# Low parts of w1 and w2 as identity products on TensorE, first score masks on VectorE

## The chip, the cores and the metric

One core of one Trainium2 chip. The metric is the device time of one execution in microseconds (us). Engines are called PE (TensorE), DVE (VectorE), ACT (ScalarE), POOL (GpSimd) and SP (SyncE, which issues loads here). Each engine works through its own queue in order.

## The reference

The input passes three stages: a gated linear attention with the delta rule, a gated product of matrices, and a soft mixture of eight experts. Cut to what is computed:

```python
k_n = k / (np.linalg.norm(k, axis=-1, keepdims=True) + 1e-06)
for t in range(S):                       # S = 768, batch 4, 8 heads, head size 48
    y[:, :, t] = einsum('bhd,bhde->bhe', q[:, :, t], state)
    v_old = einsum('bhde,bhd->bhe', state, k_n[:, :, t])
    state = state + beta[:, :, t] * einsum('bhd,bhe->bhde', k_n[:, :, t], v[:, :, t] - v_old)
x = y.transpose(0, 2, 1, 3).reshape(3072, 384)
x = ((x @ w1) * (x @ w2)) @ w3 @ w_out   # w1, w2: 384 x 1024; w3: 1024 x 1024; w_out: 1024 x 384
logits = x @ phi                         # 32 slots
slots = softmax(logits, 0).T @ x         # 4 slots for each of 8 experts
out = softmax(logits, 1) @ experts(slots)   # relu(s @ w1[e]) @ w2[e]
```

The weights w1, w2, w3 and w_out are float64.

## The kernel before, in words

**Attention.** The sequence is cut into 24 pieces of 32 positions (n), two to a pair (p), four to a solve (s). For a solve, PE makes the Gram products of the keys (`g_step`, L428), DVE masks them into `dg` (L373), transposes them (L454), takes the norms by Newton steps (L461 to L480) and inverts the 32x32 triangles by columns (L520 and L523 for the solves 0 and 1, which invert two halves of 16 and join them with PE, `join2`). `ends[s]` is the last transpose into W (L533). The score products of queries with keys go to PSUM too; `g_evac` masks them into the tile `kl`. For n below PP = 16, ACT copies the part that is masked to SBUF (`praw`, L384), POOL multiplies by the mask (L393, L400), and ACT copies four strips directly (L408). For later n, DVE masks straight from PSUM in the same lines. `chain_steps` is then the recurrence of piece n: v times norms on POOL (`pre`, L585), `ks` (L599), `vv` (L610), `yy` (L620), the state products (L630), and `xt`, which turns the result into `xT`, a high and a low part in fp32r (L645, L646).

**Weights.** The float64 values are loaded as pairs of integers (L279). `to_f32` rebuilds float32: DVE takes the exponent (L290), ACT scales it (L291), DVE puts in the sign (L292), makes the mantissa (L294, L296), and POOL multiplies the two (L299). For w1 and w2 (w12, eight blocks of 128x768, `w12_steps`) ACT casts the high part (L306) and POOL (blocks 0, 3, 6) or DVE (the others) subtracts it from the whole (L307) to give the low part. Four blocks can lie raw in SBUF, in two slots of the tile `gx` and two of `raw`; the whole has two slots (NT12). w_out and w3 go the same way in pieces of 384 or 256 columns, through the tile `hold`, with transposes on PE.

**Main.** `prod` (L695) multiplies xT by w1 and w2 in blocks f of 128 columns, 18 products of 128x256 each, `ab`; ACT copies one half (L699), DVE multiplies (L704). Logits, softmax and the sums over slots follow for each pair of pieces, then the experts.

**Order.** Steps are put down with a time (`when`, `spread`, with shifts by label in SHIFT); they are traced in order of these times, and a scheduler that simulates the engines then fixes the order of each queue. `tc.issue_after(x)` queues what is traced in its block behind x on x's own engine; it adds no wait, and does nothing to other engines' queues. An engine that waits at one instruction holds up all behind it. The PSUM banks for scores of solve 1 and for the products `ab` are the same two.

Of the kernel before, what the change touches and what calls it, by code (L numbers as in the profile page):

```python
# [42 lines left out]
DR = 0.3  # L43
NU = 2
NUG = 10
TW0 = 0.05
TW1 = 0.8
CL = 1.0
NW = 3
# [3 lines left out]
J1 = (0.8, 1.2, 1.8, 2.0)  # L53
NT12 = 2
# [7 lines left out]
LT = 1.799  # L62
LTS = 0.311
JAT = (1, 2, 3)
PP = 16
LAST = 1
EA = 11.73
JO = (-0.7, 0.1, 0.2)
G1 = -0.341
# [16 lines left out]
GA = (0.2, -0.09)  # L86
# [34 lines left out]
def kern(ctx, tc, kq, vt, kt, bl, w12, w3, wo, phi, w1e, w2e, consts, out):  # L121
# [44 lines left out]
    spr = pc.tile([128, 2, 2, 2, 32], F32R, name="spr")  # L166
    row = pc.tile([1, 32], F32, name="row")
# [74 lines left out]
    def load(p, which="kq"):  # L242
# [6 lines left out]
        SP.dma_start(out=t[64:112, 4 - i:7:2, :], in_=kq[p][64:112, 1 - i::2])  # L249
        SP.dma_start(out=t[0:64, i:4:2, :], in_=kq[p][0:64, i::2])  # L250
# [15 lines left out]
    turn, last_v = [0], []  # L266
# [15 lines left out]
    def to_f32(r, n, name):  # L282
# [79 lines left out]
    Dg = {}  # L362
# [47 lines left out]
    def g_step(n, hs, which="gp"):  # L410
# [12 lines left out]
        for h in hs:  # L423
            for b in range(4):
# [3 lines left out]
                T.matmul(gp[trow(n, b), h - hs[0]], lhsT=t[r, k[j], kc], rhs=t[r, slots, kc], start=True, stop=True)  # L428
# [6 lines left out]
        g_evac(n, hs, gp, blocks, n < PP)  # L435
# [838 lines left out]
```

## Time and profile before

| | |
|---|---|
| three runs | 642.67, 645.42, 648.51 us; median 645.42 |
| profiled execution | span 640.7 us from first to last instruction (its own time is not given beside it) |
| busy | PE 548.9 us (86%), DVE 400.3 (62%), ACT 278.6 (43%), POOL 161.8 (25%) |
| products `ab` (L695) | 1728 instructions, 247.1 us busy |
| chain of waits that ended last | PE 55%, DVE 26%, issue 6%, DMA 5%, POOL 4%, ACT 3% of the span |

The busy times are means over the whole span. The chain of waits is followed back from the last instruction: what ended each wait, or what stood ahead on the same engine. The rows below are read by stage. A time in a timeline row is the start from the first instruction, then the length of what is merged in the row; the last number is how many instructions are merged.

### The profile page before, as it was taken

Reading aid. Unit: us, or ns where it says so; the run is one execution under the profiler, and the core shown is the slowest. Engines: PE = TensorE matmul, PEld = TensorE weight load, DVE = VectorE, ACT = ScalarE, POOL = GpSimd, SP = SyncE. Lnnn points to the kernel's source line nnn. Section 1 sums busy time; section 2 is a strip of 40 time slices with the busy share of each in tenths; the row PEclk is TensorE's granted clock in tenths of the full one; section 3 lists DMA queues with packets and bytes.
Section 4 is the critical chain, followed back from the end, with each engine's and each line's share of the span. In section 5 each row is a group of like instructions: output and inputs, shape, how many; then the busy total and the mean of one; then the engine's idle time right before and its main releaser. Section 6 shows DMA issues by size and latency. Waiting matters only on the chain.

```text
span 640.7 us, 25996 instructions
## 1 busy us (share of the span) xinstructions
PE 548.9 (86%) x11417; PEld 458.8 (72%) x11417; DVE 400.3 (62%) x1257; ACT 278.6 (43%) x704; POOL 161.8 (25%) x215
## 2 busy tenths in 40 slices
PE   5324546888899799899999999897999999999996
PEld 4323435887777688679888888786989899886464
DVE  3996899998667115994379826997982313134124
ACT  1515644245574436454444455343444454333023
POOL 0726858334254016232030113004010000000100
PEclk9999666598999989999999999999999999999997
DMA  9904234446843720310404030122344130788848
GB/s 205 332 4 146 81 83 144 130 130 204 254 151 129 164 70 17 87 45 18 105 7 96 9 90 30 38 61 63 106 145 155 63 108 2 268 274 318 344 160 265
DMA packets 36945, 81.72 MB, mean 128 GB/s; under 512 B 4352, under 2 KB 17792, under 8 KB 35584
## 3 DMA queue, kind: packets, MB, share of 16 engines
q1 hardware_dynamic: 36832, 80.07, 40.9%
q8 instruction: 89, 1.46, 1.0%
q14 instruction: 24, 0.20, 0.1%
HBM read 69.57 MB, written 10.49 MB: 125 GB/s over the span
## 4 chain that ended last, share of the span: by engine, by line
PE 55%; DVE 26%; issue 6%; DMA 5%; POOL 4%; ACT 3%; SPq 0%; DVEq 0%; POOLq 0%; ACTq 0%
PE ab L695 24%; DMA kl<-kq 4%; PE gp L712 3%; PE yp L620 3%; DVE xl L512 2%; PE vp L610 2%; DVE tmp L509 2%; PE sacc L630 2%; PE gp L428 2%; PE ks L599 2%; PE sacc L1119 2%; PE hp L1098 2%; DVE gl L454 2%; DVE xl L487 1%; PE lp L719 1%
## 5 line engine op out<-in xcount | busy, mean ns | idle before, releaser
L695 PE MATMUL ab<-xT,wsl 128*128 128x256 f32 x1728 | 247.1, 296 | 3.6 <-DVE gT L704 2.2
L695 PEld LDWEIGHTS ab<-xT,wsl 128*128 128x128 f32 x1728 | 221.8, 196 | 15.6 <-issue 6.3
L704 DVE TENSOR_TENSOR gT<-ab,bs 128x256 f32<-128x256 f32 x84 | 35.2, 422 | 87.3 <-ACT bs L699 79.0
L699 ACT COPY bs<-ab 128x256 f32<-128x256 f32 x96 | 35.7, 371 | 68.0 <-PE ab L695 66.3
L585 POOL TENSOR_TENSOR v<-v,nnT 128x384 f32<-128x384 f32 x24 | 21.4, 894 | 139.2 <-DMA v<-vt 57.0
L575 ACT COPY sv<-vp 32x384 f32<-32x384 f32 x96 | 45.1, 470 | 16.2 <-PE vp L610 14.5
L512 DVE TENSOR_TENSOR xl<-xl,tmp 128x84 f32<-128x84 f32 (+35 forms) x220 | 51.5, 266 | 0.7
L509 DVE TENSOR_TENSOR tmp<-xl 128x84 f32<-128x84 f32 (+35 forms) x220 | 49.6, 259 | 0.4
L428 PE MATMUL gp<-kl 48*32 48x64 f32 (+1 forms) x1024 | 35.7, 275 | 11.7 <-ACT kl L408 8.6
L299 POOL TENSOR_TENSOR hold<-hold 128x384 f32<-128x384 f32 (+1 forms) x32 | 32.7, 1025 | 47.9 <-DVE hold L296 23.0
L428 PEld LDWEIGHTS gp<-kl 48*32 48x32 f32 x1024 | 26.1, 121 | 17.8 <-ACT kl L408 8.9
L713 ACT COPY gtok<-gp 128x512 f32<-128x512 f32 x48 | 28.2, 588 | 17.2 <-PE gp L712 15.0
L393 POOL TENSOR_TENSOR kl<-praw,cs 64x256 f32<-64x256 f32 x28 | 25.3, 903 | 33.5 <-ACT praw L384 32.3
L620 PE MATMUL yp<-sv,kl 112*32 112x48 f32 (+2 forms) x1280 | 26.3, 215 | 7.6 <-ACT sv L575 7.6
L291 ACT ACTIVATE hold<-hold,cs 128x384 int32<-128x384 int32 (+1 forms) x32 | 18.7, 589 | 27.7 <-DVE hold L290 27.3
L408 ACT COPY kl<-gp 32x256 f32<-32x256 f32 x64 | 23.2, 363 | 15.0 <-DVE kl L393 11.8
L620 PEld LDWEIGHTS yp<-sv,kl 112*32 112x32 f32 (+2 forms) x1280 | 20.4, 115 | 12.2 <-issue 8.4
L610 PE MATMUL vp<-v,w 32*32 32x48 f32 x1536 | 25.3, 207 | 3.1 <-DVE mst L738 0.9
L646 DVE TENSOR_TENSOR xT<-xp,xT 128x384 fp32r<-128x384 f32 x24 | 13.3, 553 | 22.8 <-ACT xT L645 22.6
L610 PEld LDWEIGHTS vp<-v,w 32*32 32x32 f32 x1536 | 20.1, 107 | 10.2 <-issue 6.0
L712 PE MATMUL gp<-cs,gT 128*128 128x128 f32 x168 | 26.9, 279 | 0.0
L400 POOL TENSOR_TENSOR kl<-praw,cs 32x256 f32<-32x256 f32 x28 | 23.2, 828 | 7.7 <-ACT praw L384 4.8
(248 smaller groups left out, 980.6 us busy)
## 6 DMA issues: line engine op xcount, KB each, us to landing
hold<-w SPq DMA_DIRECT2D x16, 384.0 KB, 3.3
v<-vt SPq DMA_DIRECT2D x24, 192.0 KB, 2.7
kk<-kt SPq DMA_DIRECT2D x12, 384.0 KB, 6.7
unitg<-w1e SPq DMA_DIRECT2D x6, 768.0 KB, 5.7
kl<-kq SPq DMA_DIRECT2D x8, 512.0 KB, 6.8
kl<-kq SPq DMA_DIRECT2D x8, 384.0 KB, 4.6
gx<-w SPq DMA_DIRECT2D x4, 768.0 KB, 8.2
raw_w<-w SPq DMA_DIRECT2D x4, 768.0 KB, 8.8
```

Source lines behind the costliest of these rows:

```text
L299: G.tensor_tensor(out=w, in0=m, in1=w, op=ALU.mult)
L428: T.matmul(gp[trow(n, b), h - hs[0]], lhsT=t[r, k[j], kc], rhs=t[r, slots, kc], start=True, stop=True)
L509: V.tensor_tensor(out=tmp[:, 0:n, lo:hi], in0=x[:, j + 1:32, j:j + 1].to_broadcast([128, n, hi - lo]), in1=x[:, j:j + 1, lo:hi].to_broadca ...
L512: V.tensor_tensor(out=x[:, j + 1:32, lo:hi], in0=x[:, j + 1:32, lo:hi], in1=tmp[:, 0:n, lo:hi], op=ALU.add)
L575: A.copy(o, i)
L610: T.matmul(p[o, h * D:(h + 1) * D], lhsT=w[o, 8 * n4 + h, :], rhs=r[o, h, :], start=True, stop=True, tile_position=(o.start, o.start))
L620: T.matmul(p[qrow(b), h * D:(h + 1) * D], lhsT=kl[r, (6, 0)[b // 2] if t2 else (4, 2)[b // 2], kcol(h, b)], rhs=sv[r, b, h * D:(h + 1) * D ...
L695: T.matmul(o, lhsT=w[:, m, k], rhs=x[:, k], start=(n == 0), stop=(n == 8))
L699: A.copy(bs, p[:, 256:512])
L704: V.tensor_tensor(out=gt, in0=p[:, 0:256], in1=bs, op=ALU.mult)
L712: T.transpose(p[:, t * 256 + i * 128:t * 256 + (i + 1) * 128], gt[:, t * 128:(t + 1) * 128], ident)
L713: A.copy(gk, p)
```

## The change

- `w12_steps`: the low part is no longer a subtraction. PE multiplies the whole by an identity and the high part by a negative identity (`nid`) into one PSUM bank, half a block at a time, and ACT copies the bank to the low part as fp32r.
- `to_f32`: for w12, the multiplication of blocks 0, 1, 2, 4 and 5 is done by DVE, that of 3, 6, 7 by POOL (`WG`); three blocks instead of two start together behind the first inverse (`AHEAD`), and the whole has four slots (NT12).
- Scores of the pieces 0 to 3 (`PV`) are masked by DVE from PSUM, without the copy by ACT; their steps get own times (`P0`), those after the inverse behind `solved`, the last scaling of the inverse.
- The keys of pairs 0 and 1 are loaded first, pair 1 by ACT's queue; constants and beta follow. Queries, v and the first `kk` are put down inside a block `issue_after` the last Gram product; `pre` inside one behind `solved[0]`.
- Scratch for dynamic DMA is set to 1024, and numbers that set the order are changed.

```diff
-DR = 0.3
+DR = 0.223
...
-TW0 = 0.05
+TW0 = 0.41
...
-J1 = (0.8, 1.2, 1.8, 2.0)
-NT12 = 2
+J1 = (0.8, 0.924, 1.8, 2.0)
+NT12 = 4
+AHEAD = 3
+W0 = -1.0
+W1 = -0.8
+WG = (3, 6, 7)
+PV = (0, 1, 2, 3)
+P0 = (-8.466, -0.99, -0.8, -0.6)
...
-    def to_f32(r, n, name):
+    def to_f32(r, n, name, E=G):
...
-        G.tensor_tensor(out=w, in0=m, in1=w, op=ALU.mult)
+        last_m.append(E.tensor_tensor(out=w, in0=m, in1=w, op=ALU.mult))
...
-            w = to_f32(raw_load(w12[f], 768, f"w{f}"), 768, f"w{f}")
+            w = to_f32(raw_load(w12[f], 768, f"w{f}"), 768, f"w{f}", G if f in WG else V)
             hi, lo = (wsl[f][:, i].rearrange("p m k c -> p (m k c)") for i in range(2))
             A.copy(hi, w)
-            (G if f % NW == 0 else V).tensor_tensor(out=lo, in0=w, in1=hi.bitcast(F32), op=ALU.subtract)
+            for i in range(2):
+                c = slice(384 * i, 384 * i + 384)
+                p = tr(f"lo{f}{i}")[:, 0:384]
+                T.matmul(p, lhsT=ident, rhs=w[:, c], start=True, stop=False)
+                T.matmul(p, lhsT=nid, rhs=hi[:, c], start=False, stop=True)
+                A.copy(lo[:, c], p)
...
-        g_evac(n, hs, gp, blocks, n < PP)
+        g_evac(n, hs, gp, blocks, n < PP and n not in PV)
...
+            with tc.issue_after(solved[0].ins):
+                G.tensor_tensor(out=v, in0=v, in1=nnT[s][:, 8 * n4:8 * n4 + 8].unsqueeze(2).to_broadcast([128, H, D]),
+                                op=ALU.mult)
...
-    when(-9.0, lambda: SP.dma_start(out=cs, in_=consts), *[lambda p=p: load(p, "k") for p in range(2)], lambda: load_b(0),
-         lambda: load(0, "q"), lambda: load_v(0), lambda: load_v(1), lambda: load(1, "q"), lambda: load_kk(0))
+    when(-9.0, lambda: load(0, "k"), lambda: load(1, "k", A), lambda: SP.dma_start(out=cs, in_=consts), lambda: load_b(0))
+    when(-8.89, behind_g0(lambda: load(0, "q"), lambda: load_v(0), lambda: load_v(1), lambda: load(1, "q"), lambda: load_kk(0)))
...
-    spread(-1.0, -0.8, [behind_w12(f, i - 2) for i, f in enumerate(w12s)], "w12")
+    spread(W0, W1, [behind_w12(f, i - AHEAD) for i, f in enumerate(w12s)], "w12")
...
-    nc = bacc.Bacc("TRN2", target_bir_lowering=False, num_devices=1)
+    nc = bacc.Bacc("TRN2", target_bir_lowering=False, num_devices=1, dynamic_dma_scratch_size=1024)
```

How instructions move on three queues. First SP, from its first load on, before; in brackets the semaphores that an instruction waits for (a DMAHW one is the landing of an earlier load):

```order
L862 DMA cs<-consts 128x419
L249 DMA kl_111<-kq 48x2x512
L250 DMA kl_111<-kq 64x2x512
L249 DMA kl_112<-kq 48x2x512
L250 DMA kl_112<-kq 64x2x512
L262 DMA beta_120<-bl 128x32
L249 DMA kl_111<-kq 48x2x512
L250 DMA kl_111<-kq 64x2x512
L254 DMA v_124<-vt 128x384 [waits DMAHW0_49]
```

SP with the change (`kl_112` is the tile of pair 0, `kl_113` of pair 1; line 256 and 257 are `load`):

```order
L256 DMA kl_112<-kq 48x2x512
L257 DMA kl_112<-kq 64x2x512
L891 DMA cs<-consts 128x419
L269 DMA beta_121<-bl 128x32
L256 DMA kl_112<-kq 48x2x512
L257 DMA kl_112<-kq 64x2x512
L261 DMA v_277<-vt 128x384 [waits DMAHW0_49]
L261 DMA v_279<-vt 128x384 [waits DMAHW1_49]
```

The keys of pair 1 have left the queue, the constants stand behind the keys of pair 0; the queries (the second pair of rows on `kl_112`) carry no wait, and v waits for the first landing as before.

DVE at the end of the first inverse, before:

```order
L529 TENSOR_TENSOR xf_493<-xl_489,sm_469 128x16x16 x2
L531 STREAM_TRANSPOSE sums<-xf_493 128x16x32
L533 STREAM_TRANSPOSE w_555<-xf_493 128x32x32
L290 TENSOR_SCALAR t_w_632<-gx 128x768
L290 TENSOR_SCALAR t_w_643<-raw_w_641 128x768
L292 SCALAR_TENSOR_TENSOR t_w_632<-gx,t_w_632 128x768
L292 SCALAR_TENSOR_TENSOR t_w_643<-raw_w_641,t_w_643 128x768
L294 TENSOR_SCALAR gx<-gx 128x768
L294 TENSOR_SCALAR raw_w_641<-raw_w_641 128x768
L296 SCALAR_TENSOR_TENSOR gx<-gx 128x768
```

DVE there with the change (L542 is L529 of before, L405 is L393, L297 to L303 are L290 to L296):

```order
L542 TENSOR_TENSOR xf_311<-xl_307,sm_287 128x16x16 x2
L405 TENSOR_TENSOR kl_112<-p_0_444,cs 64x256
L405 TENSOR_TENSOR kl_112<-p_4_467,cs 64x256
L544 STREAM_TRANSPOSE sums<-xf_311 128x16x32
L546 STREAM_TRANSPOSE w_373<-xf_311 128x32x32
L297 TENSOR_SCALAR t_w_533<-gx 128x768
L297 TENSOR_SCALAR t_w_551<-raw_w_549 128x768
L297 TENSOR_SCALAR t_w_570<-raw_w_568 128x768
L405 TENSOR_TENSOR kl_112<-p_0_444,cs 64x256
L405 TENSOR_TENSOR kl_112<-p_4_467,cs 64x256
L299 SCALAR_TENSOR_TENSOR t_w_533<-gx,t_w_533 128x768
L299 SCALAR_TENSOR_TENSOR t_w_551<-raw_w_549,t_w_551 128x768
```

Two masks stand ahead of the inverse's last transposes and two behind the first exponents, and three blocks are opened where two were.

ACT from the cast of block 6 on, before (L575 copies the state, L408 strips of scores, L699 the first half of `ab`):

```order
L306 CAST wsl_106<-t_w_697 128x768
L575 COPY sv<-sacc_110 48x384
L645 CAST xT_0_861<-xp_1186 128x3x128
L291 ACTIVATE hold<-hold,cs 128x384 x4
L306 CAST wsl_107<-t_w_744 128x768
L384 COPY praw_0_1250<-gp_0_1232 64x128 x2
L408 COPY kl_111<-gp_0_1232 32x2x4x32 x4
L384 COPY praw_4_1277<-gp_4_1259 64x128 x2
L408 COPY kl_111<-gp_4_1259 32x2x4x32 x4
L384 COPY praw_0_1324<-gp_0_1290 64x256 x2
L546 COPY t_2_1571<-j_2_1537 128x128
L324 COPY woT_1122<-wot_1118 128x384
```

ACT with the change (L313 is the cast, L319 the copy of a low part, L588 is L575, L396 and L420 are L384 and L408):

```order
L313 CAST wsl_107<-t_w_686 128x768
L298 ACTIVATE hold<-hold,cs 128x384 x2
L313 CAST wsl_108<-t_w_740 128x768
L319 CAST wsl_107<-lo_694 128x384
L319 CAST wsl_107<-lo_698 128x384
L588 COPY sv<-vp_936 32x384 x4
L659 CAST xT_0_973<-xp_975 128x3x128
L319 CAST wsl_108<-lo_748 128x384
L319 CAST wsl_108<-lo_752 128x384
L637 COPY ys_1014<-yp_981 128x384
L396 COPY praw_0_1037<-gp_0_1019 64x128 x2
L420 COPY kl_114<-gp_0_1019 32x2x4x32 x4
```

Between the cast of block 6 and the scores of piece 4 stand the state copies of piece 1 and the result copies now, which stood ahead of the cast before; the scores of pieces 4 and 5, which stood ahead of that cast too, come behind them.

## Rows read from the trace of the kernel before

**Rows 1.** Busy time by stage: stretch, length, then each engine's busy us and instructions.

```profile
41.10:61.80 20.70, 10.42 (x448) 8.92 (x448) 13.92 (x21) 7.87 (x13) 9.59 (x6) 1.00 0.26 88
61.80:102.50 40.70, 19.00 (x521) 15.75 (x522) 36.08 (x42) 24.17 (x52) 29.89 (x20) 0.64 0.28 78
102.50:140.30 37.80, 32.30 (x537) 29.11 (x536) 37.45 (x127) 13.24 (x29) 17.39 (x18) 0.71 0.53 164
140.30:233.00 92.70, 83.58 (x1837) 69.32 (x1837) 55.79 (x139) 46.33 (x113) 30.04 (x32) 0.94 0.56 159
233.00:585.00 352.00, 339.37 (x7027) 294.74 (x7030) 208.89 (x783) 163.46 (x424) 56.33 (x112) 1.00 0.31 92
```

**Rows 2.** Timeline of the first inverse: start, length, engine, line, operation, tiles.

```profile
14.79 1.97 DVE L454 STREAM_TRANSPOSE gl<-dg 128x1024 f32<-128x1024 f32 x1
...
27.03 0.88 DVE L523 TENSOR_TENSOR xl<-xl,sm 128x44 f32<-128x44 f32 x2
...
28.61 3.10 POOL L393 TENSOR_TENSOR kl<-praw,cs 64x256 f32<-64x256 f32 x4
...
34.99 0.33 DVE L523 TENSOR_TENSOR xl<-xl,sm 128x54 f32<-128x54 f32 x2
...
39.22 1.87 DVE L533 STREAM_TRANSPOSE w<-xf 128x1024 f32<-128x1024 f32 x1
```

**Rows 3.** Timeline, first loads on SP and PE's Gram products.

```profile
0.74 0.39 SPq L862 DMA_DIRECT2D cs<-consts  x1
...
13.53 0.70 PE L428 MATMUL g<-kl 48*32 48x32 f32 x35 [3.80 <-issue]
```

**Rows 4.** Timeline of DVE and POOL, conversion of w12.

```profile
40.93 0.54 DVE L290 TENSOR_SCALAR t_w<-gx 128x768 int32<-128x768 int32 x1
...
42.48 0.96 DVE L292 SCALAR_TENSOR_TENSOR t_w<-gx,t_w 128x768 int32<-128x768 int32 x1 [0.55 <-ACT t_w L291]
43.35 0.95 DVE L292 SCALAR_TENSOR_TENSOR t_w<-raw_w,t_w 128x768 int32<-128x768 int32 x1
...
79.03 1.85 POOL L299 TENSOR_TENSOR t_w<-raw_w,t_w 128x768 f32<-128x768 f32 x1
...
79.42 2.27 DVE L292 SCALAR_TENSOR_TENSOR t_w<-raw_w,t_w 128x768 int32<-128x768 int32 x1 [1.06 <-ACT t_w L291]
...
89.43 2.44 DVE L296 SCALAR_TENSOR_TENSOR gx<-gx 128x768 f32<-128x768 uint32 x1
...
97.86 0.95 DVE L307 TENSOR_TENSOR wsl<-t_w,wsl 128x768 fp32r<-128x768 f32 x1
```

**Rows 5.** DVE instructions grouped by shape: busy us, mean ns.

```profile
L393 DVE TENSOR_TENSOR kl<-gp,cs 64x256 f32<-64x256 f32 x12 | 5.0, 416 | 0.2
```

**Rows 6.** Timeline of PE; in brackets the idle time before and its end.

```profile
1.31 2.93 PE L816 MATMUL sacc<-sv 128*128 128x384 f32 x4 [1.31 <-DVE sv L811]
...
47.39 1.51 PE L610 MATMUL vp<-v,w 32*32 32x48 f32 x64 [0.86 <-DVE w L552]
...
98.45 1.93 PE L428 MATMUL gp<-kl 48*32 48x64 f32 x64 [7.87 <-ACT kl L408]
...
102.56 5.04 PE L695 MATMUL ab<-xT,wsl 128*128 128x256 f32 x22
...
302.17 0.88 PE L610 MATMUL vp<-v,w 32*32 32x48 f32 x64
```

**Rows 7.** Timeline of ACT: state copies, a cast of a block, strips of scores.

```profile
75.04 1.95 ACT L575 COPY sv<-vp 32x384 f32<-32x384 f32 x4
...
88.33 0.83 ACT L306 CAST wsl<-t_w 128x768 fp32r<-128x768 f32 x1
...
96.91 1.49 ACT L408 COPY kl<-gp 32x256 f32<-32x256 f32 x4
```

**Rows 8.** Timeline of DVE, first and last instruction of the second inverse.

```profile
103.74 2.04 DVE L454 STREAM_TRANSPOSE gl<-dg 128x1024 f32<-128x1024 f32 x1
...
138.06 1.92 DVE L533 STREAM_TRANSPOSE w<-xf 128x1024 f32<-128x1024 f32 x1
```

More of the change, by code (lines that the diff above doesn't have):

```diff
@@ L61 @@
 GX = 3.912
-LT = 1.799
+LT = 1.693
 LTS = 0.311
@@ L66 @@
 LAST = 1
-EA = 11.73
-JO = (-0.7, 0.1, 0.2)
-G1 = -0.341
+EA = 11.832
+JO = (-0.7, 0.007, 0.216)
+G1 = -0.437
 S1 = -0.015
@@ L85 @@
 L3 = -0.04
-GA = (0.2, -0.09)
+GA = (0.2, -0.052)
 GB = 0.203
@@ L240, in kern, with load @@
     KV, KK, bt = {}, {}, {}
-    def load(p, which="kq"):
+    def load(p, which="kq", E=SP):
         t = kl_of(p)
@@ L248, in load @@
         i = "qk".index(which)
-        SP.dma_start(out=t[64:112, 4 - i:7:2, :], in_=kq[p][64:112, 1 - i::2])
-        SP.dma_start(out=t[0:64, i:4:2, :], in_=kq[p][0:64, i::2])
+        E.dma_start(out=t[64:112, 4 - i:7:2, :], in_=kq[p][64:112, 1 - i::2])
+        E.dma_start(out=t[0:64, i:4:2, :], in_=kq[p][0:64, i::2])
     def load_v(n):
@@ L427, in g_step @@
                 slots = slice(lo, hi) if j == 0 else slice(hi - 1, lo - 1 if lo else None, -1)
-                T.matmul(gp[trow(n, b), h - hs[0]], lhsT=t[r, k[j], kc], rhs=t[r, slots, kc], start=True, stop=True)
+                m = T.matmul(gp[trow(n, b), h - hs[0]], lhsT=t[r, k[j], kc], rhs=t[r, slots, kc], start=True, stop=True)
+        last_g[:] = [m]
         blocks = {}
@@ L440, in g_parts @@
         return [lambda: g_step(2 * p, range(h)), lambda: g_step(2 * p, range(h, H)), lambda: g_step(2 * p + 1, range(H))]
-    W, nnT, ends = {}, {}, {}
+    W, nnT, ends, solved = {}, {}, {}, {}
     joined = {i: {0} for i in HALVES}
@@ L823, in behind0, with behind_x, g @@
         return g
+    def behind_x(f):
+        def g():
+            with tc.issue_after(solved[0].ins):
+                f()
+        return g
     def behind_w12(f, k):
@@ L861, in kern, with behind_g0, g @@
     w12s = w12_steps()
-    when(-9.0, lambda: SP.dma_start(out=cs, in_=consts), *[lambda p=p: load(p, "k") for p in range(2)], lambda: load_b(0),
-         lambda: load(0, "q"), lambda: load_v(0), lambda: load_v(1), lambda: load(1, "q"), lambda: load_kk(0))
+    def behind_g0(*fs):
+        def g():
+            with tc.issue_after(last_g[0].ins):
+                for f in fs:
+                    f()
+        return g
+    when(-9.0, lambda: load(0, "k"), lambda: load(1, "k", A), lambda: SP.dma_start(out=cs, in_=consts), lambda: load_b(0))
+    when(-8.89, behind_g0(lambda: load(0, "q"), lambda: load_v(0), lambda: load_v(1), lambda: load(1, "q"), lambda: load_kk(0)))
     when(-8.95, first)
+    when(-8.95, lambda: A.activation(out=nid, in_=ident, func=AF.Copy, scale=-1.0))
     for i in range(4):
@@ L867, in kern @@
                                              in_=ident4.unsqueeze(1).to_broadcast([128, 2, 32])))
-    spread(-8.9, -8.8, [lambda n=n: g_step(n, range(H), "g") for n in range(4)], "G0")
+    spread(-8.9, -8.895, [lambda n=n: g_step(n, range(H), "g") for n in range(4)], "G0")
     steps = solve_steps(0)
```

23 lines of the change are left out of this document (12 added, 11 removed).

## Prediction

> **What bounds the kernel now.** I read the stages first, then the rows inside them. The table of stages shows two halves. From 233 us to 585 us TensorE (PE) is busy 339 of 352 us: nothing but PE work sets the pace there [rows 1]. Before 140 us it is not: PE works 10.4 of 20.7 us from 41.1 to 61.8, 19.0 of 40.7 us up to 102.5, and 32.3 of 37.8 us up to 140.3, part of that at the lower clock (mean granted 0.64 and 0.71) [rows 1]. The chain of waits runs through VectorE (DVE) and GpSimd (POOL) in these stages and through PE behind them. So the start is what can be shortened; whatever point of the PE program is reached earlier by x us brings the end forward by nearly x, because behind it PE hardly waits.
>
> What sets the start, in order of time: the first inverse on DVE (14.8 to 41.1), the conversion of w1 and w2 (w12) on DVE and POOL, the first product `ab` at 102.56, the second inverse from 103.74 to 139.98 [rows 2, 6, 8].
>
> **The first inverse.** Its steps come in rows of two DVE instructions. While POOL makes the score masks (four instructions in 3.10 us from 28.61), such a row is 0.88 us long, ten of them from 27.03 to 34.99. When POOL stops, at 34.99, the same kind is 0.33 long [rows 2]. Ten rows lose 10 x (0.88 - 0.33) = 5.5 us; about five more single instructions beside the earlier masks are taken to lose 0.5 each by the same rows: 2.5. The change takes these masks from POOL, so 8.0 us go. It puts two mask instructions into the inverse ahead of the transposes: 416 ns each [rows 5], +0.8. The issue of the consts stands ahead of the keys in SP's queue, 0.39 us [rows 3]; that goes: -0.4. The inverse should end at 41.1 - 8.0 + 0.8 - 0.4 = 33.5.
>
> What does not happen: the query loads are not held back. In SP's order they wait for nothing on PE; they stand where they stood, behind the keys and beta. The Gram products stop for 3.80 us at 9.73 with no releaser shown ("issue") until 13.53 [rows 3], while the DMA queues are full. If that is instructions arriving late through the same queues, it stays; I take 0, and if the new order of loads frees it, 3.8 more. The multiplication of v by the norms is not held back either: the block names a DVE instruction, and POOL's queue is not DVE's.
>
> **The conversion of w12.** DVE per block: two tensor_scalars of 0.54 and two scalar_tensor_tensors of 0.96, of which the next starts 0.87 behind the last (42.48, 43.35) [rows 4]; less 0.08 each that is 2.67, eight blocks 21.4. The multiplication moves to DVE for five blocks, as long as the subtraction there now, 0.95 [rows 4]: 4.8. The five subtractions go. Fourteen masks come behind the inverse at 0.42 [rows 5]: 5.9. Two score and two join instructions: 1.3. Sum 33.4. POOL keeps three multiplications and one v here. Beside such a multiplication of 1.85 us a DVE instruction of 0.96 took 2.27 [rows 4]: 1.3 lost for each, 0.5 for v: 4.5. Waits for ACT and reloads, with three blocks in flight instead of two: 2, chosen. So the last block is through at 33.5 + 33.4 + 4.5 + 2 = 73.4 instead of 91.9 [rows 4], 18.5 us earlier. The Trainium skill (SBUF — State Buffer, SBUF: two separate sides) says that DVE with two SBUF inputs and POOL exclude each other for a whole instruction; by that the four POOL instructions would cost 6.4 us here instead of 4.5, and the sum would be 2 worse; the row shows less.
>
> **From there to the first product.** This does not move by 18.5. In ACT's new order, the copies that PE's next steps wait for stand behind the last two blocks' casts and low-part copies. Counted from the cast of block 6 to the last copy ahead of `ab`: two casts of a block, 0.83 each [rows 7], 1.7; four low-part copies of half a block and as many exponent steps again and two more, about 0.5 each by the cast, 5; four score evacuations of 0.5 for the raw copy and 1.49 for four strips [rows 7], 8; eight state copies, 1.95 for four [rows 7], 3.9; six smaller copies, about 0.5 each, 3. In all some 22 us with no room between; ACT starts them at about 71.5, so `ab` starts at about 93.5, where it was 102.56: -9. The load of pair 3's keys and the score bank that PE waits 7.87 us for now, until 98.45 [rows 6], come inside the same stretch. The second inverse starts at about 93 instead of 103.74: -10.7.
>
> PE gets 16 identity products of 128x384 in float32 and 16 in fp32r. The nearest row is the zeroing of the accumulators, of the same shape: 4 instructions in 2.93 us [rows 6], two to a product, so 1.46; with about 0.35 for the fp32r one 1.8, and 29 us for 16. That row runs at the lower level, as the other rows of the first 70 us do whatever the granted clock says there: 64 value products take 1.51 at 47.39 and 0.88 at 302.17 [rows 6]. At 2.4 GHz the 32 would be 14.7. PE has 20.7 + 40.7 - 29.4 = 32 us idle between 41.1 and 102.5 [rows 1]: 14.7 fits, 29 only just. I let ACT's queue hide them, at cost 0, and give the other case to a rival.
>
> **The second inverse.** Now 36.2 us [rows 8], because some six whole conversions of w_out and w3 stand among its rows, and POOL works beside it. In the new order one and two halves do. Core: the first one's 26.3 less 8.0, 18.3 [rows 2]; other DVE rows between, by the lengths above: 5. POOL works about 11 us beside it (eight masks of 0.78, five small multiplications); at the 0.55 lost per mask of 0.78 that is 6 to 8, taken as 6. So 29 us, ending at 122 instead of 140: -18. PE, whose fourth product now waits for a gate product that DVE makes only behind the inverse, no longer waits for it there. But PE must also do the 32.3 us of that stage [rows 1]. If the clock takes as long to rise as now, it needs the same 37.8 us, and the stage ends 9 earlier; at the full clock throughout it needs about 23 and DVE decides: 18 earlier. In between: 14, chosen with one more us for what PE no longer waits for: **-15**. Nothing behind changes its price: the order of the products is shifted by hundredths, and w3's conversions, moved later, fall where DVE is idle (55.8 busy of 92.7 from 140.3 [rows 1]).
>
> Against the profiled execution: its span of 640.7 becomes about 626. The median shown, 645.4, is 4.7 above that span (the runs go from 642.67 to 648.51); taken over unchanged, **630**.
>
> **Rivals.**
> - *The gain is caught on the way* (0.17). ACT or PE is late by as much as DVE is early: `ab` starts at 98 to 102. For it: ACT's 22 us have no slack and the low parts add 16 copies of 0.48 to it. Against: ACT is busy 24.2 of the 40.7 us up to 102.5 now [rows 1], so it has room while the first blocks come through. Time 641 to 645.
> - *PE becomes the bound, and the kernel is slower* (0.08). The place: the identity products stand in PE's queue ahead of the value products, and the keys of pair 3 can load only after those. At the lower clock 29.4 + 29 = 58 us from 34 on leave `ab` at 93 without any wait; each product also waits for its cast. It decides from 10 us of such waits on (there are 32 now); at half of them, 16, `ab` starts at 109 and the end is 6.5 later: 652.
> - *More than the sum* (0.23). The 3.8 us stop goes, and the denser PE work holds the upper clock from the products on: 3.8 + 18 = 22, and 28 if POOL costs the second inverse nothing either: 617 to 623. For it: PE is idle most of the time where the clock is low now. Against: up to 140.3 PE is busy 32.3 of 37.8 us and the clock still averages 0.71 [rows 1]. The Trainium skill (TensorE: Matmul & The Clock Gate, Part 1) states that the low level is the default and that activity lifts it; the rows at 47.39 and 302.17 agree [rows 6], and by it this case would be the likelier one. For the stop, the skill (Runtime: NRT & Kernel Launch, Instruction fetch mechanics) holds that fetches in blocks are mostly hidden; the 3.80 us speak against it, if it is one.
>
> **How the numbers follow.** Forecast 0.52: 9 to 19 off, 626 to 637, middle 630. A measurement here tells 1% (6.5 us) from no change. Faster by over 1% (below 639): the forecast, the last rival and a little of the first, 0.79; within 1%: 0.13; slower: 0.08. The range reaches from the deep end of the last rival taken from the lowest run, 642.67 - 28 = 614, to the top of the first, 645, and leaves out 0.08 above and some 0.05 below.
>
> **What would show it.** In the profile after: the first inverse's rows at 0.33 throughout and its end near 33; the last block near 73; ACT without gaps from 71 to 93; `ab` at 93; the second inverse ending near 122; the pause before 13.5 unchanged. It is wrong if the inverse's rows stay at 0.88 without POOL, if PE and not ACT is busy without gaps ahead of `ab`, or if the stages from 233 on grow.

## The result: 637.5 us, a gain of half the size forecast

The changed kernel takes 637.48 us (median of 4 runs, 632.80 to 639.06), the kernel before on the same chip 645.96 (4 runs). The ratio is 0.987 with a 95% interval of 0.983 to 0.991, so the change is worth 5.6 to 11 us. The forecast was 630, with a range of 614 to 645: right in direction and inside the range, but with 15 us off instead of 8.5. The profiled execution went from a span of 640.7 to 636.3. In the other profiles the time is 1.7 to 2.1 us above the span of the same execution, so that of before is of an execution of some 642.6 us, and marks compared with it show some 3 us less gain than the medians do.

### The profile page after: what moved, and what is told of

The parts are those of the page before. It is cut to its first block, busy times and chain, and to the rows that moved or that the text cites. A ratio compares the mean times of both kernels' runs of the same rounds, so it can differ in the third digit from the quotient of the medians.

```text
span 636.3 us, 26073 instructions
## 1 busy us (share of the span) xinstructions
PE 570.2 (90%) x11465; PEld 466.5 (73%) x11465; DVE 388.7 (61%) x1273; ACT 281.3 (44%) x709; POOL 126.3 (20%) x191
## 4 chain that ended last, share of the span: by engine, by line
PE 60%; DVE 23%; DMA 7%; issue 4%; ACT 3%; POOL 1%; SPq 0%; DVEq 0%; ACTq 0%; POOLq 0%
PE ab L709 25%; PE gp L440 4%; DMA kl<-kq 4%; PE gp L726 3%; PE vp L624 3%; PE lp L733 3%; PE yp L634 2%; DVE xl L525 2%; DVE tmp L522 2%; PE ks L613 2%; PE sacc L1151 2%; PE lo L317 2%; PE hp L1130 2%; PE sacc L644 1%; PE up L795 1%
## 5 line engine op out<-in xcount | busy, mean ns | idle before, releaser
L709 PEld LDWEIGHTS ab<-xT,wsl 128*128 128x128 f32 x1728 | 221.1, 195 | 18.7 <-issue 8.0
L588 ACT COPY sv<-vp 32x384 f32<-32x384 f32 x96 | 45.1, 470 | 16.2 <-PE vp L624 14.5
L440 PE MATMUL gp<-kl 48*32 48x64 f32 (+1 forms) x1024 | 38.5, 275 | 7.7 <-DMA kl<-kq 5.7
L298 ACT ACTIVATE hold<-hold,cs 128x384 int32<-128x384 int32 (+1 forms) x32 | 18.8, 590 | 28.2 <-DVE hold L297 27.0
L420 ACT COPY kl<-gp 32x256 f32<-32x256 f32 x64 | 23.2, 363 | 15.4 <-DVE kl L405 11.5
L624 PEld LDWEIGHTS vp<-v,w 32*32 32x32 f32 x1536 | 21.6, 113 | 11.4 <-issue 5.0
L624 PE MATMUL vp<-v,w 32*32 32x48 f32 x1536 | 26.8, 214 | 3.3 <-DVE v L615 3.0
L555 PE MATMUL j<-w,dg 32*32 32x16 f32 x512 | 8.6, 187 | 21.4 <-DVE w L546 17.8
L555 PEld LDWEIGHTS j<-w,dg 32*32 32x32 f32 x512 | 6.7, 113 | 24.4 <-DVE w L546 18.2
L634 PE MATMUL yp<-sv,kl 128*32 128x48 f32 (+2 forms) x1280 | 24.1, 208 | 0.1
L405 POOL TENSOR_TENSOR kl<-praw,cs 64x256 f32<-64x256 f32 x20 | 15.3, 766 | 43.1 <-ACT praw L396 42.3
```

The lines of the kernel that those rows point to most:

```text
L440: m = T.matmul(gp[trow(n, b), h - hs[0]], lhsT=t[r, k[j], kc], rhs=t[r, slots, kc], start=True, stop=True)
L588: A.copy(o, i)
L624: T.matmul(p[o, h * D:(h + 1) * D], lhsT=w[o, 8 * n4 + h, :], rhs=r[o, h, :], start=True, stop=True, tile_position=(o.start, o.start))
L634: T.matmul(p[qrow(b), h * D:(h + 1) * D], lhsT=kl[r, (6, 0)[b // 2] if t2 else (4, 2)[b // 2], kcol(h, b)], rhs=sv[r, b, h * D:(h + 1) * D ...
L709: T.matmul(o, lhsT=w[:, m, k], rhs=x[:, k], start=(n == 0), stop=(n == 8))
```

## The profile after, against the rows of before

The table of stages of the changed kernel, with the columns and stretches of [rows 1]:

```profile
41.10:61.80 20.70, 19.98 (x274) 12.15 (x275) 20.01 (x31) 11.51 (x22) 1.85 (x1) 1.00 0.46 154
61.80:102.50 40.70, 33.20 (x776) 23.67 (x776) 28.15 (x47) 27.95 (x64) 20.55 (x20) 0.79 0.38 110
102.50:140.30 37.80, 32.99 (x703) 30.03 (x702) 34.00 (x123) 13.53 (x32) 11.71 (x14) 0.86 0.30 94
140.30:233.00 92.70, 86.47 (x1909) 69.36 (x1904) 56.92 (x145) 52.27 (x135) 34.18 (x38) 0.96 0.61 171
233.00:585.00 352.00, 340.89 (x6883) 295.82 (x6885) 206.54 (x784) 156.86 (x403) 52.10 (x107) 0.98 0.31 94
```

From 41.1 to 102.5 PE is now busy 53.2 us of 61.4, where it was 29.4: the identity products lie in what was idle time. DVE's 48.2 us there were 50.0. The first inverse on DVE and what POOL does beside it (timeline, as [rows 2]):

```profile
16.56 1.97 DVE L467 STREAM_TRANSPOSE gl<-dg 128x1024 f32<-128x1024 f32 x1
...
21.96 1.61 POOL L599 TENSOR_TENSOR v<-v,nnT 128x384 f32<-128x384 f32 x2 [20.08 <-DVE nnT L495]
...
22.87 1.63 DVE L493 TENSOR_SCALAR sm<-sm 128x32 f32<-128x32 f32 x1
...
28.11 0.33 DVE L536 TENSOR_TENSOR xl<-xl,sm 128x54 f32<-128x54 f32 x2
...
32.90 0.74 DVE L405 TENSOR_TENSOR kl<-p,cs 64x256 f32<-64x256 f32 x2
...
34.52 1.86 DVE L546 STREAM_TRANSPOSE w<-xf 128x1024 f32<-128x1024 f32 x1
```

Each row of two is 0.29 to 0.34 long throughout; only beside POOL's v and the memset behind it do two small DVE instructions (128x32, 0.18 to 0.19 elsewhere) still take 0.66 and 1.63. The inverse takes 19.8 us instead of 26.3. It starts 1.8 later, though. PE's Gram products ahead of it (timeline, idle time and its end in brackets, as [rows 3]):

```profile
5.52 0.43 PE L440 MATMUL g<-kl 48*32 48x32 f32 x8 [1.28 <-DMA kl<-kq]
8.23 3.11 PE L440 MATMUL g<-kl 48*32 48x32 f32 x211 [2.28 <-DMA kl<-kq]
15.31 0.69 PE L440 MATMUL g<-kl 48*32 48x32 f32 x35 [3.97 <-issue]
```

The first eight products need only a part of pair 0's keys. The rest of them lets PE go on at 8.23 now, together with the keys of pair 1, which come by the other queue; before, pair 0 alone was there at 6.14 (timeline of before):

```profile
6.14 1.94 PE L428 MATMUL g<-kl 48*32 48x32 f32 x124 [0.83 <-DMA kl<-kq]
```

The stop without a releaser is there as before. Then the end of the conversion on DVE and POOL, the value step behind it, and PE and SP up to the first product (timeline, as [rows 4, 6]):

```profile
72.30 1.85 POOL L306 TENSOR_TENSOR t_w<-raw_w,t_w 128x768 f32<-128x768 f32 x1 [6.01 <-DVE raw_w L303]
...
72.47 2.50 DVE L303 SCALAR_TENSOR_TENSOR gx<-gx 128x768 f32<-128x768 uint32 x1
74.90 2.81 DVE L297 TENSOR_SCALAR hold<-hold 128x384 int32<-128x384 int32 x4
...
78.10 0.54 DVE L615 TENSOR_TENSOR v<-v,ks 128x384 f32<-128x384 f32 x1
78.79 0.85 PE L624 MATMUL vp<-v,w 32*32 32x48 f32 x28 [3.02 <-DVE v L615]
...
86.24 0.89 PE L634 MATMUL yp<-sv,kl 112*32 112x48 f32 x64
...
87.16 0.33 SPq L252 DMA_DIRECT2D kl<-kq  x1
...
97.52 3.62 PE L440 MATMUL gp<-kl 48*32 48x128 f32 x60 [1.30 <-DMA kl<-kq]
...
103.18 1.93 PE L440 MATMUL gp<-kl 48*32 48x64 f32 x64
105.04 2.80 PE L709 MATMUL ab<-xT,wsl 128*128 128x256 f32 x18
```

The last block is through at 75.0, 17 us earlier than in [rows 4]; the first product `ab` is at 105.04, 2.5 us later than in [rows 6]. This is where the forecast broke. The chain reads backwards: `ab` stands behind the Gram products of pair 3, those wait for that pair's keys, the keys can load only when the last reader of pair 0's keys (`yp` of piece 1, until 87.1) has freed their place. That reader is late because all of piece 1 is late. Before, its steps and that load stood here (timeline):

```profile
63.63 1.51 PE L599 MATMUL ks<-sv,kl 112*32 112x48 f32 x64
...
66.56 0.55 DVE L601 TENSOR_TENSOR v<-v,ks 128x384 f32<-128x384 f32 x1
...
67.16 0.88 PE L610 MATMUL vp<-v,w 32*32 32x48 f32 x64 [0.23 <-DVE v L601]
...
79.54 0.33 SPq L245 DMA_DIRECT2D kl<-kq  x1
```

Now `ks` of piece 1 comes at 72.61, 9.0 us later, and the subtraction that uses it starts 4.6 us behind its end (1.4 before), because the end of w12 and five steps of w_out stand ahead of it on DVE. The load is issued 7.6 us later. And it takes longer: the view of DMA issues of before, from 78 to 92 us (line, queue, KB each, median us from issue to landing),

```profile
kl<-kq SPq DMA_DIRECT2D x1, 512.0 KB, 6.6
kl<-kq SPq DMA_DIRECT2D x1, 384.0 KB, 4.5
```

and of the changed kernel, from 83 to 98 us:

```profile
hold<-wo SPq DMA_DIRECT2D x4, 384.0 KB, 5.7
wod<-hold SPq DMA_DIRECT2D x4, 192.0 KB, 4.0
kl<-kq SPq DMA_DIRECT2D x1, 512.0 KB, 9.9
kl<-kq SPq DMA_DIRECT2D x1, 384.0 KB, 7.9
```

Since w12 is done earlier, the conversions of w_out come earlier too, and their loads and stores now run where the keys load; before, none did. The four runs below that undo or add one part agree: from the first issue to the last landing this load takes 7.1 us in c and d, where no transfer of w_out runs beside it, and 9.8 and 11.3 in a and b, where they do (10.3 here, 7.0 before).

The second inverse (106.96 to 130.29) takes 23.3 us instead of 36.2 [rows 8] and ends 9.7 earlier. The third starts 2.6 earlier (240.8), the fourth 7.7 (310.4), the last product ends 5.2 earlier (574.0). Where in the work an inverse stands depends on the order; a mark that depends less on it is a count of the 1728 products `ab`. The 289th, the first of the 17th block, starts at 222.0 instead of 226.2, 4.2 earlier.

## The experiments

All were timed in 5 rounds against the kernel before on the same chip (the changed kernel in a comparison of its own). The median is that of all runs. Times in the last five columns (us) are from each one's profile: start of the first product and of the 289th, start of the third and of the fourth inverse on DVE, end of the last product.

| kernel | median | ratio to before, 95% | first `ab` | 289th | 3rd | 4th | last `ab` |
|---|---|---|---|---|---|---|---|
| before | | 1 | 102.6 | 226.2 | 243.4 | 318.1 | 579.2 |
| changed | 637.5 | 0.987 (0.983-0.991) | 105.0 | 222.0 | 240.8 | 310.4 | 574.0 |
| a_sub | 651.4 | 1.010 (1.007-1.014) | 112.5 | 229.2 | 248.9 | 326.1 | 587.6 |
| b_mask | 655.3 | 1.016 (1.012-1.019) | 109.3 | 226.1 | 245.4 | 323.0 | 587.0 |
| c_before_pe | 645.3 | 1.001 (0.999-1.004) | 101.2 | 218.0 | 237.2 | 311.8 | 579.0 |
| d_before_masks | 658.1 | 1.022 (1.018-1.026) | 110.4 | 236.7 | 250.0 | 332.5 | 594.1 |
| e_tw0 | 648.2 | 1.005 (1.002-1.008) | 108.8 | 230.9 | 249.7 | 322.7 | 584.2 |
| f_before_tw0 | 655.7 | 1.017 (1.015-1.020) | 103.7 | 237.0 | 252.7 | 327.4 | 594.3 |
| g_lo_free | 651.2 | 1.011 (1.006-1.016) | 106.4 | 224.5 | 242.7 | 323.9 | 585.4 |
| h_held | 659.0 | 1.024 (1.020-1.029) | 115.4 | 228.7 | 249.6 | 329.7 | 593.5 |
| i_old_numbers | 661.8 | 1.024 (1.021-1.027) | 119.3 | 235.2 | 257.2 | 331.6 | 602.4 |
| j_new_numbers | 649.6 | 1.006 (1.004-1.008) | 105.9 | 229.3 | 244.0 | 319.8 | 584.7 |
| k_hold_late | 645.1 | 1.000 (0.997-1.002) | 103.8 | 224.7 | 243.2 | 320.7 | 585.4 |
| n_back_old | 648.1 | 1.003 (1.000-1.007) | 104.1 | 219.7 | 234.1 | 312.2 | 584.0 |

None beats the changed kernel. A profile shows one execution: that of k took 649.7 us and that of i 666.2, above their medians, that of b 652.5 and that of c 642.3, below, so their marks can lie up to 4.6 us off what the median would give. Distances to the changed kernel are between medians on different chips; by the ratios a loses 15 us against it and b 18.

**One part undone, or one part alone.** In the changed kernel, the low parts by subtraction again:

```diff
+            (G if f % 3 == 0 else V).tensor_tensor(out=lo, in0=w, in1=hi.bitcast(F32), op=ALU.subtract)
-            for i in range(2):
...
-                A.copy(lo[:, c], p)
```

> The changed kernel with its low parts made by subtraction again (five on DVE, three on POOL, as in the kernel before); masks, loads and all numbers stay changed. Theory A, the step that failed is the price of the identity products: at the lower clock they and the waits for their copies keep value product 1, and behind it the keys of pair 3, late. Then the last block of w1 and w2 is through some 5 us later than 75.0 (five subtractions of 0.95 on DVE), but the first product comes no later than 105.0 and the kernel takes 632 to 637. Theory B, the identity products cost nothing and DVE's queue sets the first product: it moves later by the 5 us of DVE, to about 110, and the kernel takes 641 to 643 against 637.5.

The same kernel with the masks back on POOL:

```diff
-PV = (0, 1, 2, 3)
+PV = ()
...
+    spread(-8.79, -8.71, [lambda n=n, hs=hs: g_step(n, hs, "p") for n in range(4)
```

> The changed kernel with the eight pieces of the first score masks back on POOL, beside the first inverse; the rest stays changed. Theory A, the relief of the first inverse is worth its full length at the end: the inverse takes about 26 us again instead of 19.8, DVE has 14 masks of 0.42 less to do behind it, and the kernel takes 638 to 642. Theory B, what the inverse gains is absorbed before the first product anyway (by PE and the load of pair 3's keys): the first product stays at 105 and the kernel at 636 to 638.

The kernel before with the identity products alone (the first diff the other way round):

> The kernel before with one part of the change alone: low parts by identity products on PE. Theory A, PE at the lower clock is the price: the last block of w1 and w2 comes 5 to 6 us earlier than 91.9, but the first product hardly moves from 102.6 and the kernel takes 644 to 650 against 646. Theory B, PE has room: DVE loses five subtractions of 0.95 and POOL three of 1.85, and the kernel takes 639 to 642.

(The scratch for dynamic DMA is set to 1024 in it too.) And with the masks alone (the second the other way round):

> The kernel before with one part of the change alone: the first score masks on DVE, all but two of them behind the inverse. Both theories: the first inverse ends near 34 instead of 41.1. Theory A, that relief passes to the end: -7 and +3 for what of the masks DVE can't hide, 640 to 643 against 646. Theory B, it is absorbed ahead of the first product: 644 to 647.

For a, theory A is out: the first product came 7.4 us later, as B said, but the kernel lost 14 and not 5. In b the first inverse takes 26.3 us again, the first product is 4.3 later, and the kernel lost 18 where 1 to 5 was expected. c has the time of theory A but not its reason: it was 6.2 us ahead at the third inverse and had given all of it back by the last product. d took 658 where 640 to 647 was expected: its first inverse ends at 35.4 and the first product still starts 7.8 later. So each part does its work where it stands, and none gains anything by itself. And a large part of each loss arises behind the third inverse, where none of these parts has an instruction: 5.5 of 13.6 us in a and 8.4 of 13.0 in b, against the changed kernel, 8.3 of 14.9 in d and all 6 in c, against the one before. Counted from the 289th product it is 6.4 in a, 8.9 in b, 4.4 in d and 8.0 in c. That asked for the order.

**One number of the order**, TW0, which says when the conversions of w_out and w3 are due; in the changed kernel set back, in the kernel before set forward:

```diff
-TW0 = 0.41
+TW0 = 0.05
```

> The changed kernel with one number of the order set back: the conversions of w_out and w3 are due from 0.05 on again instead of 0.41, so they stand among the rows of the second inverse as before. Theory A, the gain of the change is the shorter second inverse (36.2 us before, 23.3 now), and it is short because these conversions are out of its way: the second inverse takes 30 to 36 us again and the kernel 643 to 649. Theory B, it is short because POOL is idle beside it: it stays below 26 us and the kernel at 635 to 640.

> The kernel before with that one number of the order alone: conversions of w_out and w3 due from 0.41 on. Theory A as above, but without the rest of the change: the second inverse shrinks from 36.2 to some 26 us and the kernel takes 636 to 641 against 645. Theory B, the number is worth nothing without identity products and masks: 643 to 650.

First and last row of the second inverse on DVE (timeline), in e:

```profile
110.31 1.97 DVE L467 STREAM_TRANSPOSE gl<-dg 128x1024 f32<-128x1024 f32 x1
...
153.51 1.91 DVE L546 STREAM_TRANSPOSE w<-xf 128x1024 f32<-128x1024 f32 x1
```

and in f:

```profile
104.86 2.03 DVE L454 STREAM_TRANSPOSE gl<-dg 128x1024 f32<-128x1024 f32 x1
...
128.97 1.86 DVE L533 STREAM_TRANSPOSE w<-xf 128x1024 f32<-128x1024 f32 x1
```

Theory A holds for the inverse: 45.1 us with the conversions among its rows, 26.0 without them even in the kernel before. POOL works beside it too in e (16.5 us, 6.5 in the changed kernel), as theory B has it, but that is the smaller part. Of the 21.8 us between e and the changed kernel, the 82 instructions of the inverse itself take 3.9 (22.7 against 18.8), and what stands between them on DVE takes 17.3 (21.3 against 4.0). Theory A fails for the time of f: 655.7 is above both ranges, and the third inverse starts 9.3 us later than before. A short second inverse is not by itself an early end.

**The identity products left out**, ACT's copies kept:

```diff
-                p = tr(f"lo{f}{i}")[:, 0:384]
...
-                A.copy(lo[:, c], p)
+                A.copy(lo[:, c], w[:, c])
```

> The changed kernel without the identity products on PE: ACT copies each block itself into the place of its low part, so ACT does the same 16 copies and the low parts are wrong; DVE's order stays that of the changed kernel. Theory A, the identity products at the lower clock hold up value product 1 and the keys of pair 3 (8 of them run between 79.6 and 85.5): the first product comes 5 to 9 us before 105.0 and the kernel takes 628 to 633 against 637.5. Theory B, they are hidden: 635 to 639. Theory C, they keep PE busy and its clock up (the mean granted clock from 61.8 to 80 was 0.96 with them and 0.50 in the run with subtractions): without them the value products and Gram products slow down, and the kernel takes 640 to 650.

Theory A is out: PE is busy 31.6 us from 41.1 to 102.5 instead of 53.2, yet the first product comes 1.4 us later, not earlier. The identity products were hidden. What C says of the clock is in the rows: `ks` of piece 1 here, and in the changed kernel (timeline of PE in each),

```profile
70.89 1.51 PE L610 MATMUL ks<-sv,kl 112*32 112x48 f32 x64 [1.21 <-DVE w L562]
```

```profile
72.61 0.89 PE L613 MATMUL ks<-sv,kl 112*32 112x48 f32 x64 [0.15 <-DVE w L565]
```

1.51 and 0.89 are the two lengths that 64 such small products have at 1.2 and at 2.4 GHz, as 1.51 and 0.88 of the value products in [rows 6]. The granted clock can't be read here: the first change of it that the trace of g has stands at 108.7 us, in the changed kernel at 61.6, and ahead of the first one the profile gives 1.00. The identity products themselves show the step, in the changed kernel:

```profile
45.75 2.93 PE L317 MATMUL lo<-t_w,cs 128*128 128x384 f32 x4 [0.53 <-DVE t_w L306]
...
61.61 0.91 PE L317 MATMUL lo<-t_w,cs 128*128 128x384 f32 x2
```

PE had been busy 20.0 of 20.7 us before it. The rise does not last: at the end of PE's wait of 3.02 us ahead of value product 1 (78.79, shown above) the clock falls, and it averages 0.51 from 78.6 to 85.5. So C is right for some 17 us, but its price is small: the third inverse starts 1.9 us later, and 9.5 of the 11.4 us lost by the last product arise behind it, again where the part has nothing. The time, 651.2, is just above C's range.

**The loads really held back.** ACT copies 32 elements of the last Gram bank, SP stores them, and all later loads stand behind that store:

```diff
+    def hold_back():
+        A.copy(row, last_gp[0][0:1, 0, 0, :])
+        d = SP.dma_start(out=rowd, in_=row)
+        held[:] = [d]
```

> The changed kernel with the loads behind the first keys, consts and beta really held back: ACT copies 32 elements of the last Gram product, SP stores them, and every later load of SP's queue stands behind that store. Theory A, the stop of PE in the Gram products (3.97 us until 15.31, no releaser shown) comes from full DMA queues: it shrinks below 1 us, the first inverse starts at 11 to 13 instead of 16.6, and the kernel takes 632 to 636, if the blocks of w1 and w2 still come in time. Theory B, the stop has nothing to do with the loads: it stays near 4 us, all loads come 8 us later for nothing, and the kernel takes 638 to 646.

PE's Gram products in it (timeline):

```profile
8.42 3.12 PE L442 MATMUL g<-kl 48*32 48x32 f32 x211 [2.17 <-DMA kl<-kq]
12.82 0.75 PE L442 MATMUL g<-kl 48*32 48x32 f32 x37 [1.29 <-issue]
```

With the DMA engines busy 40% of the first 14.8 us instead of 90%, the stop shrinks from 3.97 to 1.29 us and the first inverse ends at 33.1. So most of the stop goes with full DMA queues (theory A, though not below 1 us). What PE stops for is most likely its instructions. In the traces of before, of the changed kernel and of h, one packet of 16 KB runs about this time on the queue that the profile calls instruction (q8), from 10.93 to 12.09 before, 12.44 to 13.97 in the changed kernel and 10.28 to 11.53 in h. PE goes on 1.44, 1.34 and 1.29 us behind its end. In h the packet has landed when PE comes to a stop, in the two others 2.4 and 2.6 us later. But the last of the four loads of w12 that the first conversions need is issued at 26.2 instead of 18.4, an order follows in which PE waits 9.5 us for ACT's low-part copies from 62 to 82 us, and the first product is 10 us later. The 3.8 us can't be had in this way: 659.0 is above both ranges.

**Parts and numbers apart.** i has all parts and the ten old numbers of the order, j the kernel before with the ten new ones:

```diff
-DR = 0.223
-TW0 = 0.41
-J1 = (0.8, 0.924, 1.8, 2.0)
...
+DR = 0.3
+TW0 = 0.05
+J1 = (0.8, 1.2, 1.8, 2.0)
```

> The changed kernel with all its parts (identity products, masks, loads, pool of buffers) but with the numbers that set the order of the work (DR, TW0, J1, LT, EA, JO, G1, GA, SB, SHIFT) as in the kernel before. Theory A, the parts alone are the gain: 634 to 641. Theory B, parts and numbers only pay together, since each run with one thing set back so far came out 11 to 18 us above the changed kernel: 645 to 656, with the loss not ahead of the first product but behind 105 us.

> The kernel before with the new numbers of the order alone and none of the parts. If the gain is the order and not the parts: 634 to 641. If they only pay together: 645 to 660, as with the one number TW0 alone (656).

Parts alone: 2.4% slower. Numbers alone: 0.6% slower. Both: 1.3% faster. They only pay together (theory B for both), though i's 661.8 is above the range of B, and its loss is ahead of the first product too (14 of its 28 us against the changed kernel).

**Only numbers of the back half**, so that no part is touched:

```diff
-EA = 11.832
+EA = 11.73
...
-SB = -0.192
+SB = -0.124
```

and 22 entries of SHIFT, most of them hundredths.

> The changed kernel with 24 of its numbers set back to those before, all of which act behind 225 us (SHIFT of products 6 to 10, chain steps from 8 on, Gram products from 12 on and the like, SB and EA): every part of the change stays, and the order of all engines is the same up to the 17th product, at about 225 us. Theory A, what every kernel with one thing set back lost behind 240 us (8 to 12 us between the third and the fourth inverse's start, in short waits of PE and the stretches at the lower clock that follow them) is the order and not the part: up to 225 us the rows are those of the changed kernel, and the kernel takes 641 to 650 against 637.5. Theory B, the back half takes any order and the parts cost what was measured: 635 to 640.

The first product and the end of the second inverse come 0.9 us earlier than in the changed kernel, the 289th product 2.3 us earlier; the last product comes 10.0 us later. So late numbers alone, with every part in place, cost 10 us, no less than the 5.5 to 9.5 that the runs with one part undone lost behind the third inverse. That the losses of a, b, c, d and g there are of the same kind is argued from this, not shown for each. How the time is lost can be seen in the stages behind 225 us, columns as in [rows 1], n first:

```profile
225.00:250.00 25.00, 23.12 (x613) 19.09 (x611) 12.92 (x35) 15.90 (x47) 15.01 (x33) 1.00 0.11 33
250.00:260.00 10.00, 9.12 (x126) 6.63 (x126) 9.66 (x46) 3.12 (x9) 2.14 (x3) 0.83 0.08 24
260.00:312.00 52.00, 48.95 (x1069) 42.24 (x1072) 27.37 (x106) 23.86 (x60) 9.45 (x11) 1.00 0.27 61
```

with this wait of PE in the second stretch (timeline),

```profile
250.50 0.30 PE L769 MATMUL pp<-cs,pT 128*128 128x128 f32 x1 [2.36 <-DVE xT L660]
```

and the changed kernel in the same stretches:

```profile
225.00:250.00 25.00, 24.97 (x629) 20.56 (x626) 11.83 (x31) 17.21 (x51) 15.38 (x31) 1.00 0.14 46
250.00:260.00 10.00, 10.00 (x232) 8.31 (x231) 9.78 (x41) 4.04 (x11) 2.18 (x5) 1.00 0.14 34
260.00:312.00 52.00, 50.00 (x1007) 42.75 (x1002) 30.81 (x123) 24.46 (x62) 9.53 (x11) 1.00 0.26 59
```

PE, which sets the pace there, is idle 5.8 us of these 87 in n and 2.0 in the changed kernel; and in the stretch with the wait of 2.36 the granted clock averages 0.83, which costs 9.12 x (1 - 0.83) = 1.6 more, as an estimate. That is 5.4 us up to 312. Over the whole way from 225 us to the last product, idle time of PE makes 5.5 of the 10 us (16.0 against 10.5). In the other 4.4 PE is busy (343.0 against 338.6). The lower clock does not explain them: on this way n spends 13.7 us at it, the changed kernel 17.1. Their cause stays open.

**The chain to the first product.** Conversions of w_out put behind the subtraction of value 1, which stood behind them at 78.10:

```diff
+            with tc.issue_after(vsub[1].ins):
+                f()
...
-    spread(TW0, TW1, [behind_w12(f, 7) for f in wo_steps() + w3_steps()], "w3")
+    spread(TW0, TW1, [behind_v1(f) for f in wo_steps() + w3_steps()], "w3")
```

> The changed kernel with one piece of DVE's order set: the first conversions of w_out come behind the subtraction of value 1, which stood behind five of them at 78.1. Theory A, this subtraction is what keeps the first product late: it comes at 75 to 76, value product 1 some 2.5 us earlier, the keys of pair 3 too, the first product at 101 to 103 and the kernel at 633 to 636 against 637.5. Theory B, the chain waits for ACT and the load instead: the first product stays within 1 us of 105 and the kernel within 636 to 639. Theory C, the order that follows is disturbed as in the runs with one thing set back: 643 or more, the loss being behind 240.

Its chain (timeline of DVE, PE and SP):

```profile
74.43 0.54 DVE L615 TENSOR_TENSOR v<-v,ks 128x384 f32<-128x384 f32 x1
...
82.35 0.89 PE L634 MATMUL yp<-sv,kl 112*32 112x48 f32 x64
...
86.07 0.38 SPq L252 DMA_DIRECT2D kl<-kq  x1
...
96.28 3.62 PE L440 MATMUL gp<-kl 48*32 48x128 f32 x60 [3.83 <-DMA kl<-kq]
...
103.81 3.18 PE L709 MATMUL ab<-xT,wsl 128*128 128x256 f32 x18
```

The subtraction comes 3.7 us earlier, `yp` 3.9, the keys' load only 1.1, because SP's queue holds it behind two stores and a load of w_out until 86.07; it lands 10.2 us later, and PE now waits 3.83 us for it. So the first product is near theory B (1.2 us earlier, with the load and SP's queue as the limit), and the time is theory C's: from the third inverse's start to the fourth's 77.5 us instead of 69.6. One stretch of that in k (stages)

```profile
233.00:247.00 14.00, 11.66 (x326) 9.97 (x327) 6.40 (x15) 7.50 (x23) 8.08 (x12) 0.76 0.02 4
```

and a row of PE in it (timeline)

```profile
237.10 1.08 PE L440 MATMUL gp<-hold 48*32 48x128 f32 x32 [1.66 <-ACT kl L420]
```

show a wait of 1.66 us and a mean granted clock of 0.76, where the changed kernel has PE busy all 14.0 us at 1.00.

## Why the prediction was half right, step by step

- **First inverse:** right. Without POOL's masks its rows are 0.3 throughout; 19.8 us, where 26.3 - 8.0 + 0.8 = 19.1 was forecast, and b, with the masks back, takes 26.3. Its start was missed: 1.8 later instead of 0.4 earlier, by the rest of pair 0's keys, which lands with those of pair 1.
- **Query loads not held back, stop unchanged:** right (SP issues them at 3.50; 3.97 us). h_held shows what the prediction left open: the stop is mostly the full queues, and the instruction packet that lands ahead of its end makes a fetch the likely reason. The Trainium skill (Runtime: NRT & Kernel Launch, Instruction fetch mechanics) has such fetches mostly hidden; if the stop is one, 3.97 against 1.29 us with fewer loads says it is not hidden here.
- **Conversion of w12:** right: through at 75.0, forecast 73.4. From the inverse's end that is 38.6 us, forecast 39.9; the terms of that sum were not measured one by one. One was read too loosely. A DVE row beside POOL's multiplication of 1.85 does not lose a fixed 1.3: the row of 2.27 before [rows 4] ends 0.81 us behind POOL's, the one of 2.50 now (72.47) 0.82 behind. So each lost nearly all that was left of POOL's instruction, and the row of before lost less than 1.85 because POOL had begun 0.39 us ahead of it.
- **The first product, -9:** this is the step that failed; measured +2.5. The prediction took ACT's queue of 22 us as the limit and let the load of pair 3's keys "come inside the same stretch". ACT has gaps (busy 14.3 of the 22 us from 71 to 93, and 2.94 us idle ahead of 99.86), and the load is the limit: issued 7.6 us later and landing in 10.3 instead of 7.0 us, among transfers of w_out that used to come later. The prediction put the delay of piece 1, and so of the issue, at nothing without a reason. k takes away the smaller part of it, value 1 behind w_out's conversions (`yp` 3.9 us earlier); `ks`, ahead of it, stays late (72.14). In g, without identity products, it is at 70.89, so PE's added work accounts for some 1.7 of its 9.0 us; the rest is put down to the new order, which no run tests for this step. The slower load and SP's queue then keep k's product where it is.
- **Identity products at cost 0:** right as to the first product (g): PE had the room, though their rows take 18.7 and 11.9 us, about the 29 of the lower clock and not 14.7. That all rows of the first 70 us run at the lower level was read wrongly: value product 1 of before took 0.88 at 67.16, shown above. The rival that ends slower did not come.
- **Second inverse, 29 us:** 23.3, better than forecast: the 6 us taken for POOL beside it were too many. POOL works 6.5 us there, not 11, and the inverse's own instructions take 18.8, forecast 18.3. e and f show that the conversions among its rows are most of its price, and TW0 what moves them. It ends 9.7 earlier, not 18, because it starts 3.2 later, where 10.7 earlier was forecast.
- **PE, -15, and "nothing behind changes its price":** the 289th product starts 4.2 earlier, the third inverse 2.6, the last product ends 5.2 earlier; so 1.0 to 2.6 us of the gain, by the mark one takes, arise in the back half, where the prediction saw nothing. What became of the rest of the 9.7 us between the end of the second inverse and there was not taken apart. "The order of the products is shifted by hundredths": n shows that these hundredths are worth 10 us. So that the time fell inside the range is in part luck: the start gave less than forecast, and the order of the back half, which no term of the sum holds, decides over as much as the whole gain.
- **The rivals:** "caught on the way" had the right mechanism with the wrong carrier: the first product was even later than its 98 to 102, and the kernel still 1.3% faster.

What stays open: which of the 24 numbers counts, what nearly half of n's 10 us is, and why the waits of g and a behind 240 us arise; their parts and the order that fits them were not separated further.

## What to carry to other kernels

When one engine gets faster, follow the transfers that its earlier work sets off: here they collided with the one load that the next stage waited for. In a kernel whose order is fitted by numbers, undoing one part measures the part and the lost fit together; a run that changes only late numbers gives the size of the fit (10 us here, more than the whole change), and marks along the trace tell where a loss arises, if they are counts of work done and not places that the order itself moves. And a part that gains 6 us at the front (c) may have given it back before the end: read the end.

## What the runs showed of the hardware

- PE's stop without a releaser in the first Gram products goes with the load on the DMA queues: 3.97 us at a DMA share of 0.90, 1.29 at 0.40. In before, the changed kernel and h it ends 1.3 to 1.4 us behind the landing of a 16 KB packet of the instruction queue.
- Added work can lift PE's clock: `ks` of piece 1 took 0.89 us (2.4 GHz) with identity products ahead of it and 1.51 (1.2 GHz) without them. The Trainium skill (TensorE: Matmul & The Clock Gate, Part 1) says that activity lifts the clock from its low default; these rows agree. The lift is neither sure to last (granted 0.51 from 78.6 to 85.5 us, from the end of a wait of 3.02 on) nor out of reach without them (0.88 for value product 1 before).
- A short wait of PE can cost more than itself: in the stretches with the waits of 1.66 and 2.36 us the mean granted clock is 0.76 and 0.83, in the same stretches without them 1.00. In both the fall comes behind the wait, 1.6 us after it in k and 1.4 in n. The five such stretches of the changed kernel between 140 us and the last product begin in or just behind waits of 1.8 to 2.3 us. Other waits of this length had none, as one of 1.81 in the kernel before.
- A DVE row that starts while a POOL instruction runs can lose all that is left of it: seven rows of 128x768 with two inputs, 0.95 us long by themselves, ended 0.81 or 0.82 us behind the end of POOL's instruction (51.40, 57.44, 62.40, 79.42 and 89.43 before, 54.71 and 72.47 now).
